# An attention and expert network in one kernel: the rare overflow path moved to the program's end, the row selections of the first expert in another order

## The chip, the cores and the metric

The kernel runs on one core of a Trainium2 chip. The measure is the device time of one execution in microseconds (us). The core has five engines that run their own instruction queues in order and meet at semaphores: TensorE (PE in the profile; PEld is its weight load), VectorE (DVE), ScalarE (ACT), GpSimd (POOL) and SyncE (SP), which here only issues transfers.

## The reference

Three steps follow each other on 1152 tokens of width 512 (2 sequences of 576, 8 heads of 64).

```python
x = attention(q, k, v)          # 4 heads look 32 keys back, 4 at every 32nd key
logits = x @ w_gate             # 8 experts, the best one for each token
gate = softmax(logits)[best]
for token in order:             # an expert takes capacity = 1152 // 8 * 2 = 288 tokens
    keep it if counts[best] < capacity
out1 = gate * (relu(x @ w1[best]) @ w2[best])     # 0 for tokens not kept
out = (sigmoid(out1 @ w_gate2) * (out1 @ w_val)) @ w_out    # 512 -> 1536 -> 512
```

## The kernel before, in words

**Attention and routing.** Twenty units of attention (`attend(i)`) pass through the engines in four stages, their inputs loaded five units ahead. Each finished group of token tiles (128 tokens) is routed (`route_group`, groups of 4, 2, 1, 2 tiles): the best expert, the token's place within that expert's list (a matmul with a triangle of ones and the running counts `accb`), and a write of the token's number into the list `slist` by GpSimd. `route_consts` copies small tables from the second load of constants; it runs after the fourth unit.

**The rows of the first expert** are not gathered from memory but selected on TensorE: `pick_first(t)` multiplies a tile's rows with a 0/1 mask `first` that VectorE makes, and adds into four PSUM tiles `hot`. The rows of the first four tiles are gathered by GpSimd into `xs0` and added by a multiplication with the unit matrix (`pick_first(0)`). The sums are copied to `xd`, split into a rounded high part and a remainder. All matmuls of the expert network work on such pairs: high times high and remainder in one pass of 384 columns, low weight times high in one of 192.

**The expert network** works on `W0` = 192 rows per expert. Its order is written out by hand in `slots`: 64 blocks, four of the first layer ("a", two PSUM halves each) and four of the second ("b") for each expert; the first expert's four "a", then its four "b", from the second expert on an "a" of the next expert between two "b". A block is 16 matmuls. Behind each block the loop emits the evacuation of the block before (`evac`: ScalarE copies one half, VectorE adds the other, ScalarE writes the high part, VectorE the remainder), and the split of a weight chunk four blocks ahead (`split_hi`). "b" blocks are evacuated in pairs of two quarters of the model width. PSUM has four pairs of banks in turn. In the last four blocks the loop also runs steps of `ahead`, which brings the first two pieces of the second network's weights from 64 bits to pairs.

**The overflow path.** An expert with more than 192 tokens has its further rows (up to 96) computed in `overflow`. `values_load` reads the largest count into a register of every engine, and `tc.If(most > W0)` skips the body with a jump. For this input the body is skipped. It stands ahead of the first expert's blocks; it adds its rows into `x2h` and `x2l`, the input of the second network, which the experts then write at offsets `offs` taken from `off_i`. The counts and offsets (`count_offsets`) are made at the seam between routing and experts.

**The second network** makes gate and value for twelve pieces of 128 columns and three token groups of 384 (lines 993 to 995), then multiplies with the output weights tile by tile (nine tiles, lines 1008 to 1010); ScalarE copies a tile out and GpSimd scatters its rows (line 105) by the token list `list_sb`.

Of the kernel before, what the change touches and what calls it, by code (L numbers as in the profile page):

```python
# [20 lines left out]
P = 128  # L21
# [9 lines left out]
WARM = (6, 1)  # L31
AHEAD = 5
# [8 lines left out]
def moe_net_kernel(ctx, tc, cap, S, cst, un, wgate, w1, w2, wgv, wo, out):  # L41
# [51 lines left out]
    tails = list(range(W0, cap, W0))  # L93
    off_i = const.tile([1, E * (1 + len(tails)) + 1], I32, name="off_i")
# [130 lines left out]
    def busy(n):  # L225
        for _ in range(n):
            nc.tensor.matmul(out=warm, lhsT=idle[:, 0:P], rhs=idle, start=True, stop=True)
# [226 lines left out]
    soff = const.tile([P, E], F32, name="soff")  # L454
    mxc = const.tile([P, 1], F32, name="mxc")
    cnt = const.tile([P, E], F32, name="cnt")
    t64 = const.tile([P, E, E], F32, name="t64")
    tne = const.tile([P, NT, E], F32, name="tne")
    cpf = const.tile([P, NT], F32, name="cpf")
    cpi = const.tile([P, NT], I32, name="cpi")  # L460

    def count_offsets():
        cp = ps_tile("ps_o")
        nc.tensor.matmul(out=cp[:, 0:E], lhsT=ones_bf, rhs=accb, start=True, stop=True)
        yield
        nc.vector.tensor_copy(out=cnt, in_=cp[:, 0:E])
        nc.vector.tensor_reduce(out=mxc, in_=cnt, axis=AX.X, op=ALU.max)
        nc.vector.tensor_copy(out=off_i[0:1, E:E + 1], in_=mxc[0:1, :])
        yield
        nc.vector.tensor_tensor(out=t64, in0=below,  # L470
                                in1=cnt.unsqueeze(1).to_broadcast([P, E, E]), op=ALU.mult)
        nc.vector.tensor_reduce(out=soff, in_=t64, axis=AX.X, op=ALU.add)
        nc.vector.tensor_copy(out=off_i[0:1, 0:E], in_=soff[0:1, :])
        for i, c0 in enumerate(tails):
            nc.vector.tensor_scalar(out=off_i[0:1, E + 1 + i * E:E + 1 + (i + 1) * E], in0=soff[0:1, :], scalar1=float(c0),
                                    scalar2=float(N), op0=ALU.add, op1=ALU.min)

    def list_places():
        nc.vector.tensor_tensor(out=tne, in0=oh_all, in1=soff.unsqueeze(1).to_broadcast([P, NT, E]), op=ALU.mult)
        nc.vector.tensor_reduce(out=cpf, in_=tne, axis=AX.X, op=ALU.add)  # L480
        nc.vector.tensor_tensor(out=cpi, in0=cpf, in1=rank_all, op=ALU.add)
# [659 lines left out]
```

## Time and profile before

| | |
|---|---|
| median of three runs | 480.5 us (479.15 to 482.31) |
| profiled execution | 480.65 us, its span 478.9 us |
| TensorE busy | 452.0 us, 94% of the span |
| VectorE, ScalarE, GpSimd busy | 321.6, 241.0, 103.6 us |
| mean granted TensorE clock | 0.972 of full |

The profile is of one execution. Its view of stretches gives, for a piece of the span, how long each engine was busy and which clock TensorE was granted; the timeline gives instructions in order of time, and behind an instruction how long its engine stood idle before it and who released it ("issue" where no releaser shows). A busy TensorE need not run at its full clock.

### The profile page before, as it was taken

Reading aid. Unit: us, or ns where it says so; the run is one execution under the profiler, and the core shown is the slowest. Engines: PE = TensorE matmul, PEld = TensorE weight load, DVE = VectorE, ACT = ScalarE, POOL = GpSimd, SP = SyncE. Lnnn points to the kernel's source line nnn. Section 1 sums busy time; section 2 is a strip of 40 time slices with the busy share of each in tenths; the row PEclk is TensorE's granted clock in tenths of the full one; section 3 lists DMA queues with packets and bytes.
Section 4 is the critical chain, followed back from the end, with each engine's and each line's share of the span. In section 5 each row is a group of like instructions: output and inputs, shape, how many; then the busy total and the mean of one; then the engine's idle time right before and its main releaser. Section 6 shows DMA issues by size and latency. Waiting matters only on the chain.

```text
span 478.9 us, 7652 instructions
## 1 busy us (share of the span) xinstructions
PE 452.0 (94%) x2777; PEld 427.6 (89%) x2777; DVE 321.6 (67%) x625; ACT 241.0 (50%) x513; POOL 103.6 (22%) x97
## 2 busy tenths in 40 slices
PE   7899968699999999999979999999999999999994
PEld 3698867699999999999979999999999998888883
DVE  5489772267787877878778888888888872312110
ACT  4688742256787677767535433434444431313120
POOL 3433613334453844420300000000000000101010
PEclk9899997699999999999989999999999999999998
DMA  8988070497859978768434333334443100101001
GB/s 213 356 241 323 3 275 24 89 325 246 224 202 237 289 227 251 239 201 263 150 115 133 130 125 113 121 127 133 133 131 130 46 1 0 45 22 43 24 27 39
DMA packets 25360, 72.03 MB, mean 150 GB/s; under 512 B 6629, under 2 KB 7013, under 8 KB 25314
## 3 DMA queue, kind: packets, MB, share of 16 engines
q1 hardware_dynamic: 22946, 66.21, 43.6%
q0 software_dynamic: 2368, 5.24, 3.5%
q8 instruction: 24, 0.39, 0.4%
q14 instruction: 22, 0.18, 0.1%
HBM read 65.94 MB, written 5.79 MB: 150 GB/s over the span
## 4 chain that ended last, share of the span: by engine, by line
issue 49%; PE 29%; POOL 2%; DMA 1%; ACT 1%; POOLq 0%; DVE 0%; ACTq 0%
PE ps_p L770 28%; POOL out_dram L105 2%; PE ps_t L752 1%; DMA list_sb<-tlist 1%; POOL wlo L180 0%; POOLq L1137 0%; ACT bs L788 0%; ACT whi L176 0%; DVE ps_p L789 0%; DVE hd L799 0%; ACT hd L793 0%; POOLq L105 0%; POOLq L945 0%; ACTq L788 0%; POOLq L180 0%
## 5 line engine op out<-in xcount | busy, mean ns | idle before, releaser
L993 PE MATMUL ps_q<-x2h,whi 128*128 128x384 f32 x264 | 88.2, 334 | 0.0
L994 PE MATMUL ps_q<-x2l,whi 128*128 128x384 f32 x264 | 88.2, 334 | 0.0
L995 PE MATMUL ps_q<-x2h,wlo 128*128 128x384 f32 x264 | 88.2, 334 | 0.0
L770 PE MATMUL ps_p<-hd,whi 128*128 128x384 f32 x256 | 76.6, 359 | 0.7 <-DVE hd L799 0.7
L176 ACT ACTIVATE whi<-raw 128x1024 fp32r<-128x1024 f32 x60 | 63.5, 1059 | 4.8 <-PE ps_p L770 4.4
L182 DVE TENSOR_TENSOR wlo<-raw,whi 128x1024 fp32r<-128x1024 f32 x52 | 65.5, 1259 | 0.3 <-ACT whi L176 0.3
L770 PE MATMUL ps_p<-hd,wlo 128*128 128x192 f32 x256 | 59.6, 253 | 0.0
L105 POOL DMA_INDIRECT out_dram<-ob,list_sb x9 | 8.8, 980 | 231.4 <-ACT ob L1012 231.4
L993 PEld LDWEIGHTS ps_q<-x2h,whi 128*128 128x128 f32 x264 | 49.6, 188 | 0.0
L994 PEld LDWEIGHTS ps_q<-x2l,whi 128*128 128x128 f32 x264 | 49.6, 188 | 0.0
L995 PEld LDWEIGHTS ps_q<-x2h,wlo 128*128 128x128 f32 x264 | 49.6, 188 | 0.0
L770 PEld LDWEIGHTS ps_p<-hd,whi 128*128 128x128 f32 x256 | 47.8, 189 | 0.9 <-DVE hd L799 0.9
L770 PEld LDWEIGHTS ps_p<-hd,wlo 128*128 128x128 f32 x256 | 48.2, 190 | 0.0
L770 PE MATMUL ps_p<-xd,whi 128*128 128x384 f32 x128 | 41.4, 383 | 5.7 <-issue 5.7
L971 DVE TENSOR_TENSOR wlo<-gv,whi 128x768 fp32r<-128x768 f32 x18 | 16.4, 955 | 44.8 <-ACT whi L970 44.8
L1010 PE MATMUL ps_q<-woh,wlo 128*128 128x512 f32 x108 | 42.0, 389 | 0.0
L1009 PE MATMUL ps_q<-wol,whi 128*128 128x512 f32 x108 | 42.0, 389 | 0.0
L1008 PE MATMUL ps_q<-woh,whi 128*128 128x512 f32 x108 | 42.0, 389 | 0.0
L180 POOL TENSOR_TENSOR wlo<-raw,whi 128x512 fp32r<-128x512 f32 x16 | 26.6, 1685 | 63.3 <-ACT whi L176 63.2
L789 DVE TENSOR_TENSOR ps_p<-ps_p,bs 128x384 f32<-128x384 f32 x48 | 27.0, 562 | 17.8 <-ACT bs L788 16.3
L770 PE MATMUL ps_p<-wol,whi 128*128 128x384 f32 x128 | 37.7, 354 | 0.0
L671 ACT ACTIVATE whi<-mag 128x512 fp32r<-128x512 f32 x22 | 14.0, 635 | 46.0 <-DVE mag L669 46.0
(147 smaller groups left out, 917.3 us busy)
## 6 DMA issues: line engine op xcount, KB each, us to landing
raw<-in_w_dram SPq DMA_DIRECT2D x64, 512.0 KB, 5.2
raw<-in_wgv_dram SPq DMA_DIRECT2D x24, 512.0 KB, 3.5
raw<-in_wo_dram SPq DMA_DIRECT2D x12, 512.0 KB, 3.5
un<-in_un_dram SPq DMA_DIRECT2D x8, 672.0 KB, 7.9
xrows<-xra SPq DMA_DIRECT2D x13, 256.0 KB, 6.1
un<-in_un_dram SPq DMA_DIRECT2D x12, 172.0 KB, 4.9
un<-in_un_dram SPq DMA_DIRECT2D x8, 190.0 KB, 4.1
un<-in_un_dram SPq DMA_DIRECT2D x2, 352.0 KB, 9.0
```

What stands on the lines that cost most here:

```text
L105: ins = nc.gpsimd.indirect_dma_start(in_offset=None, oob_is_err=False, **kw)
L176: nc.scalar.activation(out=hi, in_=raws[j], func=AF.Copy)
L180: nc.gpsimd.tensor_tensor(out=lo[:, sl], in0=raws[j][:, sl], in1=hi[:, sl].bitcast(F32), op=ALU.subtract)
L182: lo_next.append(lambda: nc.vector.tensor_tensor(out=lo, in0=raws[j], in1=hi.bitcast(F32), op=ALU.subtract))
L770: nc.tensor.matmul(start=i == 0 and j == 0, stop=i == n - 1 and j == 1, skip_group_check=True, **kw)
L789: nc.vector.tensor_tensor(out=top, in0=top, in1=bs, op=ALU.add)
L993: nc.tensor.matmul(out=pq[:, 0:TG], lhsT=whv[:, k, fs], rhs=x2h[:, k, gs_], start=k == 0, stop=False)
L994: nc.tensor.matmul(out=pq[:, 0:TG], lhsT=whv[:, k, fs], rhs=x2l[:, k, gs_], start=False, stop=False)
L995: nc.tensor.matmul(out=pq[:, 0:TG], lhsT=wlv[:, k, fs], rhs=x2h[:, k, gs_], start=False, stop=k == ND - 1)
L1008: nc.tensor.matmul(out=pq, lhsT=hv[:, k, :], rhs=woh[:, f, :], start=f == 0, stop=False)
L1009: nc.tensor.matmul(out=pq, lhsT=hv[:, k, :], rhs=wol[:, f, :], start=False, stop=False)
L1010: nc.tensor.matmul(out=pq, lhsT=lv[:, k, :], rhs=woh[:, f, :], start=False, stop=f == NF2 - 1)
```

## The change

The overflow path becomes independent of the main path and moves behind the last tile's matmuls, ahead of the last two output copies: it computes its rows through both networks and scatters them itself. So that nothing of it is needed earlier, `x2h` and `x2l` are filled with zeros in the first four blocks (ScalarE and VectorE), the token numbers in the list are pushed out of range for tokens beyond place 192 (`tok2`), and counts and offsets are made behind the first block. The selection from `xs0` is put last; eight matmuls of zeros are put ahead of the last group's ranks and four behind the last selection. `route_consts` runs after the eighth unit. The first two pieces of the second network are loaded and split earlier, and the last two quarters of the last expert are evacuated one by one.

```diff
+SEAM = (8, 4)
...
-    extras = {3: route_consts, 5: fills}
+    extras = {5: fills, 7: route_consts}
...
     until(g3, "pe")
+    spin = ps_tile("ps_t")
+    busy(SEAM[0], spin)
     until(g3, "acc")
     until(g2)
-    pick_first(0)
     pick_first(N0 + 2)
-    counts = count_offsets()
-    next(counts)
     until(g3)
     pick_first(N0 + 3, N0 + 4)
-    next(counts)
+    pick_first(0)
+    busy(SEAM[1], spin)
...
-    if cap > W0:
-        most = nc.values_load(off_i[0:1, E:E + 1], min_val=0, max_val=N, skip_runtime_bounds_check_because=why)
-        overflow(ps_pair("ps_l"), most)
...
-            out_pp = (kind, e, c, y_pp) if c % 2 else None
+            if e == E - 1 and c >= ND - 2:
+                out_pp = (kind, e, [c], y_pp)
+            else:
+                out_pp = (kind, e, [c - 1, c], y_pp) if c % 2 else None
+        if i == 0:
+            count_offsets()
+        if i < ND and cap > W0:
+            nc.scalar.activation(out=x2h[:, i, 0:N], in_=ones_bf[:, 0:1].to_broadcast([P, N]), func=AF.Copy, scale=0.0)
+            nc.vector.memset(x2l[:, i, 0:N].bitcast(F32), 0.0)
         ev = evac(*done, wmain) if done else iter(())
...
-        if i == 4:
+        if i == 2:
             list_places()
...
-        if kind == "b" and e == E - 1:
-            for _ in range((6, 6, 2, 0)[c]):
-                next(ahead, None)
+        left = len(slots) - i
+        if left in (13, 12):
+            wide_loads(14 - left)
+        for _ in range((0, 2, 2, 2, 2, 2, 1, 1)[left - 1] if left <= 8 else 0):
+            next(ahead, None)
...
+        obs.append((t, pq))
+        if t == NT - 1 and cap > W0:
+            most = nc.values_load(off_i[0:1, E:E + 1], min_val=0, max_val=N, skip_runtime_bounds_check_because=why)
+            overflow()
+        if t != NT - 2:
+            while obs:
+                store_out()
```

How the instructions stand: TensorE at the seam, from the end of the last group's ranks, first before (`xs_93` is the gathered `xs0`, `first` the masks).

```order
L411 LDWEIGHTS ones_bf
L411 MATMUL ps_o<-ohb,ones_bf 128x8
L500 MATMUL ps_s<-front,xs_93 128x96 x6
L500 MATMUL ps_t<-front,xs_93 128x96 x2
L500 MATMUL ps_s<-first,xra 128x192 x3
L500 MATMUL ps_t<-first,xra 128x192
L464 LDWEIGHTS ones_bf
L464 MATMUL ps_o<-accb,ones_bf 128x8
L500 MATMUL ps_s<-first,xra 128x192 x6
L500 MATMUL ps_t<-first,xra 128x192 x2
L883 TENSOR_LOAD off_i
L838 COMPARE_AND_BRANCH
```

And with the change.

```order
L413 LDWEIGHTS ones_bf
L413 MATMUL ps_o<-ohb,ones_bf 128x8
L473 MATMUL ps_s<-first,xra 128x192 x3
L473 MATMUL ps_t<-first,xra 128x192
L473 MATMUL ps_s<-first,xra 128x192 x6
L473 MATMUL ps_t<-first,xra 128x192 x2
L473 MATMUL ps_s<-front,xs_93 128x96 x6
L473 MATMUL ps_t<-front,xs_93 128x96 x2
L229 LDWEIGHTS idle
L229 MATMUL ps_t<-idle 128x512
```

The rows from `xs0` stand behind the three tiles, the count matmul is gone, and matmuls of zeros stand where the register load and the jump were.

VectorE from the start of the first expert's blocks, before: weight splits (`wlo`), the sums (`ps_p`) and remainders (`hd`) of the first evacuations.

```order
L168 TENSOR_TENSOR wlo<-raw,whi 128x512 x2
L789 TENSOR_TENSOR ps_p<-ps_p,bs 128x2x192
L182 TENSOR_TENSOR wlo<-raw,whi 128x1024
L799 SCALAR_TENSOR_TENSOR hd<-ps_p,hd 128x2x192
L789 TENSOR_TENSOR ps_p<-ps_p,bs 128x2x192
L799 SCALAR_TENSOR_TENSOR hd<-ps_p,hd 128x2x192
L789 TENSOR_TENSOR ps_p<-ps_p,bs 128x2x192
L182 TENSOR_TENSOR wlo<-raw,whi 128x1024
L799 SCALAR_TENSOR_TENSOR hd<-ps_p,hd 128x2x192
```

And with the change, from the count's copy on, up to the remainder of the first block (lines 793, 184 and 803 are those of 789, 182 and 799 before).

```order
L622 COPY cnt<-ps_c 128x8
L623 TENSOR_TENSOR t_1191<-below,cnt 128x64
L625 TENSOR_REDUCE soff<-t_1191 128x8
L626 CAST off_i<-soff 1x8
L627 TENSOR_REDUCE mxc<-cnt 128x1
L628 CAST off_i<-mxc 1x1
L869 MEMSET x2l 128x1152
L170 TENSOR_TENSOR wlo<-raw,whi 128x512
L869 MEMSET x2l 128x1152
L793 TENSOR_TENSOR ps_p<-ps_p,bs 128x2x192
L184 TENSOR_TENSOR wlo<-raw,whi 128x1024
L803 SCALAR_TENSOR_TENSOR hd<-ps_p,hd 128x2x192
```

Six small operations for the offsets and two fills stand ahead of the first block's evacuation.

ScalarE at the end of the expert network, before, from the first piece of the second network (`mag`, `woh`) on; `bs` and `x2h` belong to evacuations.

```order
L652 ACTIVATE mag<-raw 128x512
L671 ACTIVATE woh<-mag 128x512
L652 ACTIVATE mag<-raw 128x512
L671 ACTIVATE woh<-mag 128x512
L788 ACTIVATE bs<-ps_p 128x384
L796 ISA
L796 ACTIVATE x2h<-ps_p 128x2x192
L788 ACTIVATE bs<-ps_p 128x384
L796 ISA
L796 ACTIVATE x2h<-ps_p 128x2x192
```

And with the change.

```order
L653 ACTIVATE mag<-raw 128x512
L792 ACTIVATE bs<-ps_p 128x384
L800 ISA
L800 ACTIVATE x2h<-ps_p 128x2x192
L673 ACTIVATE woh<-mag 128x512
L792 ACTIVATE bs<-ps_p 128x192
L800 ISA
L800 ACTIVATE x2h<-ps_p 128x192
L792 ACTIVATE bs<-ps_p 128x192
L800 ISA
L800 ACTIVATE x2h<-ps_p 128x192
```

The two pieces no longer stand together ahead of an evacuation, and the last two quarters are copied with 192 columns each.

## Rows read from the trace of the kernel before

**Rows 1.** The chain of waits, one of four alike (start us, us, what).
```profile
148.78 18.26 PE ps_p L770 x128
```
**Rows 2.** The waits between 15 and 45 us (us in total, times, longest).
```profile
DVE below L251 <- DMA cs<-in_cst_dram: 2.9, 1, 2.9
...
PE ps_t L319 <- POOL pt L310: 1.9, 1, 1.9
```
**Rows 3.** Stretches: length, busy us of PE, PEld, DVE, ACT, POOL; PEclk; DMA share; GB/s.
```profile
20.00:24.00 4.00, 4.00 (x31) 3.46 (x32) 1.56 (x6) 2.58 (x12) 2.61 (x6) 0.73 1.03 318
...
74.00:76.00 2.00, 2.00 (x11) 2.00 (x11) 0.00 (x0) 0.00 (x0) 1.59 (x2) 0.50 0.02 1
...
88.00:90.00 2.00, 2.00 (x8) 1.68 (x7) 0.60 (x1) 0.21 (x1) 0.00 (x0) 0.50 0.25 14
...
96.00:98.00 2.00, 2.00 (x11) 2.00 (x11) 0.35 (x1) 0.88 (x2) 1.77 (x2) 0.68 1.01 367
...
249.00:250.00 1.00, 1.00 (x5) 1.00 (x5) 0.97 (x3) 0.67 (x2) 0.00 (x0) 0.50 0.00 0
...
380.00:440.00 60.00, 60.00 (x292) 52.90 (x291) 21.93 (x30) 16.29 (x26) 3.97 (x4) 1.00 0.05 18
```
**Rows 4.** The timeline at the seam: start us, us, engine, line, operation [idle before <-releaser].
```profile
71.63 0.67 DVE L435 TENSOR_SCALAR first<-cs,sl,gs 128x192 f32<-128x192 f32 x2
...
72.53 2.70 PE L500 MATMUL ps_s<-front,xs 96*128 96x96 f32 x12 [3.43 <-DMA xs<-xrows,idx]
...
81.40 0.81 PE L500 MATMUL ps_t<-first,xra 128*128 128x192 f32 x4
...
83.47 0.15 DVE L475 TENSOR_SCALAR off_i<-soff 1x8 int32<-1x8 f32 x1
...
86.63 0.63 ACT L166 ACTIVATE whi<-raw 128x512 fp32r<-128x512 f32 x1 [2.83 <-issue]
...
87.05 0.69 PE L770 MATMUL ps_p<-xd,whi 128*128 128x384 f32 x1 [4.83 <-issue]
...
90.85 0.69 PE L770 MATMUL ps_p<-xd,whi 128*128 128x384 f32 x1 [0.82 <-issue]
```
**Rows 5.** Prices: timeline at the start, groups of VectorE, the page's groups.
```profile
1.20 2.74 PE L227 MATMUL ps_t<-idle 128*128 128x512 bf16 x6 [1.20 <-DVE zt L221]
...
L198 DVE MEMSET un<- 64x216 f32 x4 | 1.0, 238 | 0.3
...
L220 DVE MEMSET idle<- 128x256 uint32 x1 | 0.3, 272 | 0.9 <-PEq L1130 0.9
...
L176 ACT ACTIVATE whi<-raw 128x1024 fp32r<-128x1024 f32 x60 | 63.5, 1059 | 4.8 <-PE ps_p L770 4.4
L182 DVE TENSOR_TENSOR wlo<-raw,whi 128x1024 fp32r<-128x1024 f32 x52 | 65.5, 1259 | 0.3 <-ACT whi L176 0.3
```
**Rows 6.** The timeline where the first expert's first layer ends.
```profile
101.89 0.49 ACT L788 ACTIVATE bs<-ps_p 128x384 f32<-128x384 f32 x1 [0.52 <-PE ps_p L770]
...
104.15 0.44 PE L770 MATMUL ps_p<-hd,whi 128*128 128x384 f32 x1 [0.68 <-DVE hd L799]
```
**Rows 7.** The timeline between the two networks.
```profile
243.97 0.36 PE L770 MATMUL ps_p<-hd,whi 128*128 128x384 f32 x1
246.99 0.44 PE L993 MATMUL ps_q<-x2h,woh 128*128 128x384 f32 x1 [2.65 <-ACT x2h L796]
...
250.92 0.34 PE L995 MATMUL ps_q<-x2h,wol 128*128 128x384 f32 x1
...
244.58 0.63 ACT L671 ACTIVATE woh<-mag 128x512 fp32r<-128x512 f32 x1 [2.79 <-DVE mag L669]
245.12 0.47 ACT L788 ACTIVATE bs<-ps_p 128x384 f32<-128x384 f32 x1
```
**Rows 8.** The timeline's last instruction, and the drains of the program's last line.
```profile
473.38 0.97 POOL L105 DMA_INDIRECT out_dram<-ob,list_sb  x1 [7.19 <-ACT ob L1012]
...
L1137 POOLq DRAIN  x3: 46/113/4875, 473.1 to 478.6; - x3
```
**Rows 9.** DMA issues between 50 and 110 us, the last number median us to landing.
```profile
slist<-tok_i,si POOLq DMA_INDIRECT x8, 4.3
...
slot_sb<-slist SPq DMA_DIRECT2D x1, 9.0 KB, 4.4
```

More of the change, by code (lines that the diff above doesn't have):

```diff
@@ L92, in moe_net_kernel @@
     xd = wp.tile([P, ND, 2, W0], F32R, tag="xd", name="xd", bufs=1)
-    tails = list(range(W0, cap, W0))
-    off_i = const.tile([1, E * (1 + len(tails)) + 1], I32, name="off_i")
+    CT = cap - W0
+    assert CT <= 96
+    off_i = const.tile([1, E + 1], I32, name="off_i")
     ZR = -(-(E * cap) // P)
@@ L223, in moe_net_kernel, with busy @@
     warm = ps_tile("ps_t")
-    def busy(n):
+    def busy(n, at=None):
         for _ in range(n):
-            nc.tensor.matmul(out=warm, lhsT=idle[:, 0:P], rhs=idle, start=True, stop=True)
+            nc.tensor.matmul(out=warm if at is None else at, lhsT=idle[:, 0:P], rhs=idle, start=True, stop=True)
     busy(WARM[0])
@@ L452, in route_group @@
                 yield
[L454 to L481, printed above, removed]
     picked = []
@@ L626, in moe_net_kernel @@
     after(ins, slots_puts)
-    for _ in counts:
-        pass
     attn.close()
@@ L658, in narrow_steps @@
         lw, hw = rv[:, :, 0], rv[:, :, 1]
[L659 removed]
+        if wd is None:
+            wd = m2a.tile([P, 512], U32, tag="wd", name="wd", bufs=1)
         nc.vector.tensor_scalar(out=wd, in0=hw, scalar1=5, scalar2=2,
@@ L783, in moe_net_kernel, with evac @@
     where = {s: i for i, s in enumerate(slots)}
-    def evac(kind, e, c, pp, w):
-        top = pp[:, :, 0:w]
-        bs = mk.tile([P, 2, W0], F32, tag="bs", name="bs", bufs=3)[:, :, 0:w]
-        nc.scalar.activation(out=bs, in_=pp[:, :, w:2 * w], func=AF.Copy)
+    def evac(kind, e, cs_, pp, w):
+        n = len(cs_)
+        s0 = cs_[0] % 2
+        top = pp[:, s0:s0 + n, 0:w]
+        bs = mk.tile([P, 2, W0], F32, tag="bs", name="bs", bufs=3)[:, 0:n, 0:w]
+        nc.scalar.activation(out=bs, in_=pp[:, s0:s0 + n, w:2 * w], func=AF.Copy)
         nc.vector.tensor_tensor(out=top, in0=top, in1=bs, op=ALU.add)
@@ L912, in moe_net_kernel @@
                 mm_pair(wmain, [(whv[:, k, fs], wlv[:, k, fs], xds[e][:, k]) for k in range(ND)], last_pp[:, q])
-            out_pp = (kind, e, c, last_pp)
+            out_pp = (kind, e, [c * NQ1 + q for q in range(NQ1)], last_pp)
         else:
@@ L999, in moe_net_kernel, with store_out, out_mms @@
     gv_pend.pop()()
-    for t in range(NT):
-        if t + 1 < NT:
-            gsp[t + 1] = gv_split(t + 1)
-        parts = gsp.pop(t)
-        pq = ps_tile("ps_q")
+    obs = []
+    def store_out():
+        t, pq = obs.pop(0)
+        ob = m2a.tile([P, D], F32, tag="mag", name="ob")
+        nc.scalar.activation(out=ob, in_=pq, func=AF.Copy)
+        put(out_puts, "out", out=out, out_offset=bass.IndirectOffsetOnAxis(ap=list_sb[:, t:t + 1], axis=0), in_=ob,
+            bounds_check=N - 1)
+    def out_mms(pq, parts):
         for f in range(NF2):
@@ L1017, in _units @@
+    for t in range(NT):
+        if t + 1 < NT:
+            gsp[t + 1] = gv_split(t + 1)
+        pq = ps_tile("ps_q")
+        out_mms(pq, gsp.pop(t))
+        obs.append((t, pq))
[5 more added lines that the diff above has]
+                store_out()
 def _units(B, S):
```

182 lines of the change are left out of this document (113 added, 69 removed).

## The prediction

> **What bounds the kernel now.** I read the view of stretches first. From 104 us to 244 us and from 251 us to 472 us TensorE is never idle: in the first, eight blocks of weights take 18.26 us, 2.28 us each, and the chain of waits shows only such rows [rows 1]; in the second it is busy in 60.00 of 60 us [rows 3]. Work taken off another engine in these stretches is worth nothing. What can be won lies where TensorE waits, or runs at its lower clock: three places, which I then read in the timeline. In the first, at 12 to 22 us, VectorE stands 2.9 us for the second load of constants, TensorE then 1.9 us for GpSimd's product, which hangs on VectorE [rows 2]; behind it the granted clock falls: 0.73 of full over 20 to 24 us, so at half (1.2 GHz of 2.4) for some 2.2 us of it [rows 3]. The second is the seam between the routing and the first expert. TensorE waits 3.43 us for the gathered rows `xs0`, runs the row selections at half clock, ends them at 82.2 us, and begins the first expert only at 87.05 us; a second hole of 0.82 us follows before 90.85 us [rows 4]. Half clock stands at 74 to 76 us, at 88 to 90 us, and until about 97 us [rows 3]. The third is the seam between the two networks: the last weight matmul of the experts ends at 244.33 us, the next one begins at 246.99 us, and eleven matmuls from there take 3.93 us [rows 7] at half clock [rows 3].
>
> **The change, part by part.** The profiled execution took 480.65 us (span 478.9 us), 0.15 us from the median of the three times, so the sum is made against 480.65 us.
>
> *Constants later (first place).* The five copies and memsets of `route_consts` move from the fourth to the eighth unit, when their load has long landed. VectorE no longer stands 2.9 us; TensorE's wait of 1.9 us behind it goes [rows 2], and with it, as I take it, the half clock behind that wait, worth up to 1.1 us. What is late next is the units' own loads: the DMA share is full there [rows 3], so part is given back. I take **-2.5 us**; the ends are 0 (the loads bind) and -3.5 us. The five operations cost nothing at their new place, where VectorE waits for scores between units.
>
> *The seam up to the first expert.* Two things leave it. The register load, compare and jump over the overflow body: ScalarE shows 2.83 us for them, TensorE 4.83 us, which includes 1.4 us until VectorE's last write of the offsets at 83.62 us [rows 4]. And the wait for `xs0`: the selection from `xs0` now stands last, behind those of the last three tiles. I follow TensorE. Six fillers took 2.74 us at the program's start, as long as 512 columns take at half clock, so 0.45 us each [rows 5]; I take 0.21 us at full clock. Eight of them, 1.7 us, now stand ahead of the rank matmuls of the last group, which ended at 69.1 us (72.53 less 3.43 us, [rows 4]); less the short wait that stood there, these come 1.5 us later. VectorE's count update waits for them and comes 0.9 us later, and so do the masks behind it: the first of the last three at about 71.9 us, the last two, which were done at 72.3 us, at 73.2 us [rows 4]. Three tiles follow, eight passes and about 1.3 us each (four passes take 0.81 us with the tail of the last, [rows 4]): one from 71.9 us, two from 73.2 us, to 75.9 us. Of the sixteen passes from `xs0` twelve took 2.70 us at half clock [rows 4], so all take some 1.8 us at full clock, to 77.6 us, then four fillers to 78.5 us. The first two quarters of the rows are copied out behind the eighth pass, before 78 us. So the first expert begins at 78.5 us and not 87.05 us: 8.5 us.
>
> *The first expert.* What is not needed at the seam now stands here, in front of evacuations. VectorE gets four memsets of 1152 columns, the six offset operations, and five list operations after block 2 in place of three after block 4; ScalarE gets four fills. Two memsets of [rows 5] give 0.85 ns for each further column, so 1.03 us each; ScalarE's 1024 columns take 1.06 us [rows 5], so about 1.17 us each. The Trainium skill (VectorE: DVE Perf Modes, Zero memsets can be issued as uint32 (trn2), and Specifications) gives a memset one cycle per element at 0.96 GHz: by that 1.20 us each and an end 0.7 us later; the rows say 1.03 us, and the sum goes by them. Each of these operations stands ahead of the evacuation of the block before on its queue. VectorE: the count matmul is out at 80.9 us; then offsets 1.3 us (six of some 0.2 us), memset 1.0, half a split 0.6, memset 1.0, sum 0.5, split 1.15 [rows 5], remainder 0.5 and handovers: block 0 is evacuated at 87.1 us. In the same way block 1 at 89.6, block 2 (behind lists, memset, split) at 93.9, block 3 at 95.4 us. TensorE ends blocks 0 to 2 at 85.4 us. Block 3 needs the PSUM pair of block 0 (the count tile takes one of four) and runs 87.1 to 89.4 us. The next block, the first of the second layer, needs the evacuations one by one: half of it to 90.5 us, its third quarter at 93.9 us, its end at 96.0 us. Before, its last quarter began at 104.15 us behind the same chain from ScalarE's copy to VectorE's remainder, 2.3 us long [rows 6], so it ended at 104.7 us. So of the seam **-8.7 us** is left here. The ends: -13.7 us if the added operations hid entirely (78.5 plus five blocks plus the 1.1 us of the last chain), and -5 us if the clock is at half through the selections (3.7 us of them come back). The chain is nearest to the first value, since it is made of rows.
>
> *The clock behind it.* TensorE now waits 1.7 us before block 3 and 3.4 us inside the next. After 1.9 us, 2.66 us and 3.43 us of waiting this trace fell to half [rows 2, 3, 4, 7]; at 103.5 us after 0.7 us it didn't. So part of the following blocks runs at half: 3 us of it costs 1.5 us. I take **+1.5 us**; the ends are 0 and +4.5 us, the latter from the 9 us of half clock behind 87 us.
>
> What follows is covered: the last list write, at about 77.5 us, lands 4.3 us later, the slot table 4.4 us after that [rows 9], the gathers for the second expert at about 94 us; they are wanted at 102 us.
>
> *The seam between the networks.* The two early gate pieces are split at the last eight blocks, not in the last four, and each of the last two quarters is evacuated alone. Now, ScalarE's copy at 245.12 us stood behind a split that waited for VectorE [rows 7]. Then, three quarters are ready when the blocks end, and the first 18 matmuls of the second network need no more; the last quarter's four operations of 192 columns (some 1.6 us with handovers) lie under them. Gone are 2.66 us of waiting and half of 3.93 us. I take 0.2 us off: **-4.4 us**; the ends are -2.5 us (if the splits, of which two steps now stand ahead of a hidden-layer evacuation, hold TensorE for a block) and -4.7 us. The two early loads take two of the four load buffers; the weights behind them come about a block later, and their splits have four blocks to spare.
>
> *The end.* The jump stands before the last two output copies. ScalarE, VectorE, SyncE and GpSimd reach it with 8 us of TensorE's last tile to go, so their jumps are hidden. TensorE's comes after its last matmul, some 4.8 us, beside GpSimd's last scatter and the drain of 4.88 us that the end waits for [rows 8]: **0 us**, with +3 us as the far end.
>
> Sum: -2.5 - 8.7 + 1.5 - 4.4 = -14.1 us, **466.5 us**.
>
> **The rivals.**
> *The clock is lost at the seam.* The fillers don't hold it, the selections run at half and the first expert's stalls draw another 9 us of it: the seam brings 5 us and the clock takes 3 us: 480.65 - 2.5 - 5 + 3 - 4.4 = 471.7 us. For it: the masks still leave TensorE 1.2 us without work at 70.7 us. Against: 0.7 us did no harm.
> *The price of the jump moves to the end.* If TensorE's jump, or GpSimd's wait for all its scatters before it, is on the path, 2.8 to 4.8 us come back: 470.3 us. For it: every engine paid it at the seam. Against: the hiding worked out above. The Trainium skill (Runtime: NRT & Kernel Launch, Instruction fetch mechanics) says that a jump beyond what is prefetched stalls the engine for a fetch, wherever it stands; the 2.83 us of ScalarE agree, and what counts is who waits.
> *It doesn't do all it says.* The unit loads bind at the start (0) and the splits hold the last blocks (-2.5): 480.65 - 7.2 - 2.5 = 470.9 us.
> *Slower.* VectorE stays behind after the first expert, TensorE is interrupted in block after block and stays at 1.2 GHz, where each block costs 2.28 us more. Without the 1.5 us above the sum stands at 465 us; from the seventh such block on the kernel is slower, with ten it takes 487.8 us. For it: VectorE arrives some 5 us late and is busy most of the time. Against: a block at half clock takes 4.6 us, twice VectorE's work, so it would catch up in two or three.
>
> **How the numbers follow.** The forecast has 0.55 (463.5 to 469.5 us by itself), the lost clock 0.20, the jump 0.08, the partial effect 0.13, slower 0.04. The range reaches from 462 us (all ends good but the hidden fills) to 473 us, over the three milder rivals. About 1% (4.8 us) is what a measurement of this kernel tells from no change: faster than 475.8 us has 0.89, with 0.07 for a sum of several bad ends within 1%, and 0.04 slower.
>
> **What would show it.** Right: no wait of VectorE for constants and a clock of 1.00 at 20 to 24 us; the first weight matmul of the experts some 10 us earlier; clock 1.00 in the selections; TensorE waits before block 3 and in the first second-layer block, released by VectorE; no hole between the networks; the drain at the end as long as before. Wrong: half clock at the selections, an end that waits for TensorE's jump, or memsets far from 1.03 us, of which each 0.5 us on all four moves the sum by 1.5 to 2 us.

## The result, and the profile after

The changed kernel took 469.6 us (median of four runs, 469.32 to 469.81), the kernel before beside it 481.36 us (479.15 to 482.31): a ratio of 0.9762, with a 95% interval of 0.9724 to 0.98. The profiled execution took 469.32 us, its span is 467.5 us against 478.9 us. The same kernel was measured twice more, in later groups of runs, each group on a chip of its own beside the kernel before: 476.16 us (472.18 to 477.46, ratio 0.9881, 0.9809 to 0.9954) and 475.5 us (471.6 to 476.75, ratio 0.9913, 0.9885 to 0.9941). So the change is faster in all three, as each interval lies below 1: by 2.4% in the first and by about 1% in the others. Most of the experiments ask what makes this difference between the first measurement and the later two.

Two views of the profile after answer to rows of before. The first is the view of stretches: from:to, length, busy time (and instructions) of TensorE, its weight loads, VectorE, ScalarE and GpSimd, granted clock, DMA share, GB/s.

```profile
16.00:20.00 4.00, 3.86 (x38) 3.52 (x40) 2.42 (x10) 3.91 (x22) 2.11 (x4) 1.00 1.03 400
20.00:24.00 4.00, 3.83 (x40) 3.35 (x38) 3.57 (x11) 2.96 (x16) 2.83 (x7) 1.00 1.04 312
74.00:76.00 2.00, 2.00 (x19) 1.89 (x18) 0.38 (x1) 0.79 (x3) 1.70 (x2) 1.00 0.02 1
90.00:92.00 2.00, 0.00 (x0) 0.00 (x0) 2.00 (x3) 1.70 (x3) 1.58 (x2) 0.92 0.70 203
92.00:94.00 2.00, 1.17 (x4) 1.03 (x4) 1.44 (x4) 0.82 (x2) 1.80 (x2) 0.50 0.55 145
94.00:96.00 2.00, 1.80 (x8) 1.58 (x7) 2.00 (x2) 0.10 (x1) 1.69 (x2) 0.50 0.23 82
96.00:98.00 2.00, 2.00 (x9) 2.00 (x8) 1.79 (x2) 0.95 (x1) 0.00 (x0) 0.50 0.65 156
98.00:100.00 2.00, 2.00 (x13) 2.00 (x13) 0.21 (x1) 0.54 (x1) 0.00 (x0) 0.88 0.95 377
```

The clock of 0.73 at 20 to 24 us [rows 3] is 1.00, and so is the one in the selections (74 to 76 us, 0.50 before). What is left of half clock (1.2 GHz) stands at 92 to 98 us, behind a stretch in which TensorE does nothing and VectorE is busy all the time.

The second view is the timeline of the changed kernel at four places: start, duration, engine and line, output and input, count, and in brackets the idle time before and what ended it.

```profile
68.86 0.17 DVE L420 TENSOR_TENSOR accb<-accb,cn 128x8 bf16<-128x8 bf16 x1 [0.47 <-PE ps_o L413]
...
74.03 1.48 PE L473 MATMUL ps_s<-front,xs 96*128 96x96 f32 x12
75.09 0.78 ACT L593 ACTIVATE xd<-ps_s 128x384 fp32r<-128x384 f32 x2 [2.68 <-PE ps_s L473]
...
76.88 0.44 PE L772 MATMUL ps_p<-xd,whi 128*128 128x384 f32 x1
...
81.01 1.02 DVE L869 MEMSET x2l<- 128x1152 f32 x1 [0.40 <-issue]
...
85.28 0.55 DVE L803 SCALAR_TENSOR_TENSOR hd<-ps_p,hd 128x384 fp32r<-128x384 f32 x1
...
88.66 0.44 PE L772 MATMUL ps_p<-hd,whi 128*128 128x384 f32 x1 [1.72 <-DVE hd L803]
...
89.36 0.17 DVE L638 TENSOR_TENSOR tok<-far,tok_i 128x9 int32<-128x9 f32 x1
...
92.23 0.55 DVE L803 SCALAR_TENSOR_TENSOR hd<-ps_p,hd 128x384 fp32r<-128x384 f32 x1
...
92.83 0.69 PE L772 MATMUL ps_p<-hd,whi 128*128 128x384 f32 x1 [3.36 <-DVE hd L803]
...
93.16 2.53 POOL L182 TENSOR_TENSOR wlo<-raw,whi 128x512 fp32r<-128x512 f32 x2
...
94.29 2.49 DVE L184 TENSOR_TENSOR wlo<-raw,whi 128x1024 fp32r<-128x1024 f32 x1
...
236.54 0.36 PE L772 MATMUL ps_p<-hd,whi 128*128 128x384 f32 x1
236.74 0.34 PE L945 MATMUL ps_q<-x2h,woh 128*128 128x384 f32 x1
...
238.15 0.44 PE L945 MATMUL ps_q<-x2h,woh 128*128 128x384 f32 x1 [0.20 <-ACT x2h L800]
...
460.47 0.39 PE L967 MATMUL ps_q<-woh,wlo 128*128 128x512 f32 x1
460.94 0.60 ACT L957 ACTIVATE ob<-ps_q 128x512 f32<-128x512 f32 x1 [7.56 <-PEq L991]
461.81 0.97 POOL L107 DMA_INDIRECT out_dram<-ob,list_sb  x1 [7.19 <-ACT ob L957]
```

At the first seam TensorE goes from the selections to the first expert at 76.88 us (87.05 us before [rows 4]). In the first expert it waits 1.72 and 3.36 us for VectorE's remainders `hd` (0.68 us once before [rows 6]). Between the networks the hole of 2.65 us [rows 7] is gone: 0.20 us. The last scatter goes out 5.7 us ahead of the end; it was 5.5 us in the kernel before [rows 8].

To compare kernels whose first 60 us differ from run to run, I cut each trace at six events: VectorE's last count update (`accb`, 68.86 us above), the first weight matmul of the experts (76.88), the transposes of the second expert (101.57), the last weight matmul of the experts (236.54), the last matmul (460.47) and the end of the span (467.47). A is from the first to the second, B, C, D and E the next ones, in us, all of the one execution whose trace is kept; "time" is the median of the runs. That execution was the slowest of its kernel in e4, e5 and e6 (477.84, 477.46 and 475.13 us) and the fastest in e3 and e9 (474.79 and 471.6 us), so a trace and a median need not agree.

| kernel | count update | A | B | C | D | E | time |
|---|---|---|---|---|---|---|---|
| before | 69.88 | 17.17 | 22.35 | 134.58 | 228.06 | 6.83 | 481.36 |
| changed | 68.86 | 8.01 | 24.70 | 134.97 | 223.92 | 7.00 | 469.6 |
| e1, no fills | 68.59 | 10.50 | 20.32 | 135.07 | 223.91 | 6.83 | 466.97 |
| e2, fills on GpSimd | 71.23 | 10.31 | 19.78 | 134.99 | 223.91 | 6.83 | 469.46 |
| e3, no filler | 67.01 | 10.61 | 29.48 | 135.04 | 223.93 | 6.83 | 476.17 |
| e4, constants early | 70.00 | 10.59 | 29.62 | 135.04 | 223.91 | 6.83 | 473.78 |
| e5, changed again | 69.19 | 10.49 | 29.91 | 134.94 | 223.91 | 7.23 | 476.16 |
| e6, before without jump | 71.26 | 14.12 | 17.42 | 134.58 | 229.10 | 6.81 | 472.94 |
| e7, xs0 early | 69.00 | 12.49 | 27.25 | 134.99 | 223.93 | 7.22 | 475.62 |
| e8, old second seam | 68.52 | 10.28 | 29.88 | 134.56 | 227.88 | 7.14 | 479.59 |
| e9, changed, third time | 67.38 | 10.45 | 26.15 | 135.09 | 223.91 | 6.83 | 475.5 |
| e10, relieved | 69.05 | 10.31 | 20.70 | 135.04 | 223.91 | 6.83 | 467.75 |
| e11, relieved, xs0 in the middle | 69.85 | 10.20 | 21.47 | 135.09 | 223.91 | 6.83 | 469.28 |
| e12, relieved, no filler | 68.43 | 11.03 | 20.23 | 135.08 | 223.93 | 6.82 | 466.82 |

The groups are e1 to e4 (the kernel before beside them 479.2 us), e5 to e8 (480.27 us) and e9 to e12 (480.0 us). From before to after the span lost 11.4 us: 1.0 before the count update, 9.2 in A, 4.1 in D; B gave back 2.4, C 0.4, E 0.2. Among the others only A and B differ much, but for D in e8, which undoes the second seam, and in e6, where it is 1.0 us longer than before.

### The profile page after: what moved, and what is told of

Its sections match the earlier page's. It is cut to its first block, busy times and chain, and to the rows that moved or that the text cites. A ratio compares the mean times of both kernels' runs of the same rounds, so it can differ in the third digit from the quotient of the medians.

```text
span 467.5 us, 7692 instructions
## 1 busy us (share of the span) xinstructions
PE 448.8 (96%) x2789; PEld 423.6 (91%) x2789; DVE 328.1 (70%) x632; ACT 244.8 (52%) x519; POOL 103.2 (22%) x97
## 4 chain that ended last, share of the span: by engine, by line
issue 47%; PE 37%; DVE 5%; DMA 5%; POOL 3%; ACT 2%; POOLq 0%; SPq 0%; DVEq 0%; ACTq 0%
PE ps_p L772 26%; DMA out_dram<-ob,list_sb 3%; PE ps_s L288 3%; PE ps_t L321 1%; PE ps_s L473 1%; POOL out_dram L107 1%; PE ps_x L368 1%; PE ps_o L335 1%; PE ps_t L754 1%; DMA list_sb<-tlist 1%; DVE x2l L869 1%; DMA un<-in_un_dram 1%; PE ps_o L348 1%; POOL pt L312 1%; ACT pt L299 1%
## 5 line engine op out<-in xcount | busy, mean ns | idle before, releaser
L772 PE MATMUL ps_p<-hd,whi 128*128 128x384 f32 x256 | 79.3, 368 | 5.4 <-DVE hd L803 5.3
L184 DVE TENSOR_TENSOR wlo<-raw,whi 128x1024 fp32r<-128x1024 f32 x52 | 66.7, 1283 | 0.2 <-ACT whi L178 0.2
L772 PE MATMUL ps_p<-hd,wlo 128*128 128x192 f32 x256 | 60.6, 257 | 0.0
L772 PEld LDWEIGHTS ps_p<-hd,whi 128*128 128x128 f32 x256 | 49.1, 194 | 6.5 <-DVE hd L803 6.5
L772 PEld LDWEIGHTS ps_p<-hd,wlo 128*128 128x128 f32 x256 | 49.6, 196 | 0.0
L772 PE MATMUL ps_p<-xd,whi 128*128 128x384 f32 x128 | 37.6, 355 | 0.1
L957 ACT ACTIVATE ob<-ps_q 128x512 f32<-128x512 f32 x9 | 5.4, 598 | 56.5 <-issue 30.5
```

What stands on the lines that cost most here:

```text
L184: lo_next.append(lambda: nc.vector.tensor_tensor(out=lo, in0=raws[j], in1=hi.bitcast(F32), op=ALU.subtract))
L772: nc.tensor.matmul(start=i == 0 and j == 0, stop=i == n - 1 and j == 1, skip_group_check=True, **kw)
```

## The experiments

**e1, the fills left out.** The rows that they zero are all written by an expert with these inputs.

```diff
-        if i < ND and cap > W0:
-            nc.scalar.activation(out=x2h[:, i, 0:N], in_=ones_bf[:, 0:1].to_broadcast([P, N]), func=AF.Copy, scale=0.0)
-            nc.vector.memset(x2l[:, i, 0:N].bitcast(F32), 0.0)
```

> The changed kernel without the eight zero fills of x2h and x2l (left out: the zeroing of rows that no expert writes; with these inputs no such row exists). Theory A, the fills queued ahead of the first expert's evacuations are what the seam gives back: four memsets of 1.02 us on VectorE and the handovers behind ScalarE's fills go, the waits of 1.72 and 3.36 us in the first second-layer block shrink to under 2 us in all, the clock behind it stays up or falls for a shorter time, and the time is 4 to 6 us less, 463.5 to 465.5 us. Rival B, VectorE is late through its weight splits and evacuations anyway (about 2.3 us of them for each block of 2.28 us) and the offset and list operations: the waits stay at 4 us or more and the time is 468 to 469.5 us.

466.97 us (466.54 to 467.07), ratio 0.9742 (0.9714 to 0.977). B is 20.32 us, 4.4 us less than in the changed kernel's own trace and 9.6 us less than in e5's. The waits for `hd` come to 2.1 us for 5.3 us, just over theory A's 2 us. Theory A holds in the stretch that it speaks of; the time came out 1.5 us above its range, and A (the table's) was 2.5 us longer, for a reason that e5 looks into.

**e2, the fills on GpSimd.**

```diff
+    if cap > W0:
+        for i in range(ND):
+            for x in (x2h, x2l):
+                nc.gpsimd.memset(x[:, i, 0:N].bitcast(F32), 0.0)
     fetch(1)
     fetch(2)
```

> The changed kernel with the eight fills as eight memsets on GpSimd, which stands idle from 76.1 to 88.4 us, instead of four on VectorE and four on ScalarE. From the 0.96 us that GpSimd's memset of 96x1024 took, 1.08 us each, 8.6 us in all, out by about 85 to 88 us. Theory A: as without the fills, 463.5 to 466 us. Rival C, GpSimd's memsets slow VectorE's operations beside them or run past 88.4 us and hold the row gathers behind them: VectorE's splits take over 1.3 us for 1.21 us or the second expert's transposes wait, and 467 us or more is left.

469.46 us (467.59 to 470.51), ratio 0.9795 (0.9754 to 0.9835). B is 19.78 us, as without the fills, and eight memsets of 1.06 to 1.09 us on GpSimd leave VectorE's split beside them at 1.20 us. So moving them is as good as leaving them out where they stood. The time is 2.5 us above e1's; in the two traces (1.8 us apart) the count update comes 2.64 us later, and A and B are 0.7 us shorter. The code ahead of it is the same, but for the fillers, in eleven of these traces, and there it comes at 67.0 to 71.2 us. So C falls for the stretch, and the time alone decides neither.

**e3, no filler matmuls.**

```diff
-SEAM = (8, 4)
+SEAM = (0, 0)
```

> The changed kernel without the twelve filler matmuls (8 ahead of the last ranks, 4 behind the last selection). Theory A, the fillers hold TensorE's clock through the wait for VectorE's masks: without them the granted clock falls to half between 68 and 78 us, the selections take up to twice their 0.10 us a pass, and the time is 2 to 4 us more, 471.5 to 473.5 us. Rival D, the order of the selections alone keeps the pauses short and the fillers are only work on the path: the time is 0.5 to 2 us less, 467.5 to 469 us.

476.17 us (474.79 to 476.62), ratio 0.993 (0.9904 to 0.9956). The clock is 1.00 until 76 us and then 0.62 and 0.53, so it did not fall in the selections. A plus B is 40.1 us, in e5, with the fillers and with the same long A, 40.4 us. The time is that of e5. That speaks for D, though not for its 0.5 to 2 us less; e12 asks again. In this timeline one list operation of VectorE took 2.83 us (0.22 us in the changed kernel), and it ended with GpSimd's split:

```profile
91.37 2.83 DVE L634 TENSOR_TENSOR tne<-oh_all,soff 128x72 f32<-128x72 f32 x1
...
91.57 2.52 POOL L182 TENSOR_TENSOR wlo<-raw,whi 128x512 fp32r<-128x512 f32 x2
```

**e4, the constants early again.**

```diff
-    extras = {5: fills, 7: route_consts}
+    extras = {3: route_consts, 5: fills}
```

> The changed kernel with the five constant operations back behind the fourth unit. Theory A, that move brought 1.57 us (the product of the first group's last rows 66.11 to 64.54 us): VectorE stands some 2.9 us for the constants at 15 to 18 us, the clock falls to 0.7 over 20 to 24 us, and the time is 471.0 to 471.5 us. Rival E, the 1.57 us came from other moves ahead of 64 us or are absorbed later: 469.3 to 470 us.

473.78 us (472.25 to 477.84), ratio 0.9876 (0.9833 to 0.9919). VectorE stands 2.5 us for the constants, and the stretches show the clock of before:

```profile
16.00:20.00 4.00, 2.22 (x18) 2.01 (x15) 2.66 (x10) 3.37 (x18) 2.31 (x3) 0.84 1.04 393
20.00:24.00 4.00, 4.00 (x33) 3.26 (x33) 1.95 (x6) 2.19 (x10) 2.17 (x5) 0.73 1.04 295
```

So the mechanism is the one expected. Its size can't be had from this time: A and B are as in e5, and the runs are 5.6 us apart. The count update comes at 69.88, 70.00 and 71.26 us in the three traces with the constants early, at 67.01 to 71.23 us, on average 68.83 us, in the eleven with them late: 1.5 us, within a spread of 4 us. The fillers stand ahead of this event and take part of the gain back: from the count update before it to this one it is 2.77 us in the changed kernel and 2.2 us in the four traces without fillers. At the last matmuls ahead of the fillers (the products with the gate weights, 66.11 us before, 64.54 us in the changed kernel) the gain is 1.57 us, on average over the same traces 1.8 us.

**e5, the changed kernel again.**

> The changed kernel once more, unchanged, beside the others of this group. In the four traces of the first group ScalarE's copy of the first expert's rows began 2.3 to 2.5 us after the selections' passes as the trace has them (in the changed kernel's own trace 0.05 us after). Theory F, that pause belongs to the run or the chip and not to the edits: it shows here too, the first weight matmul stands near 79 us, and the time is 469 to 474 us with a wide spread. Rival G, the edits brought it: no pause, first weight matmul near 76.9 us, 469.3 to 469.9 us.

476.16 us (472.18 to 477.46). The pause shows, and then a second difference that I had not foreseen, both in its timeline:

```profile
74.39 1.48 PE L473 MATMUL ps_s<-front,xs 96*128 96x96 f32 x12
...
75.70 0.61 PE L473 MATMUL ps_t<-front,xs 96*128 96x96 f32 x4
...
77.92 0.71 ACT L593 ACTIVATE xd<-ps_s 128x384 fp32r<-128x384 f32 x2 [5.15 <-PE ps_t L229]
...
79.68 0.42 PE L772 MATMUL ps_p<-xd,whi 128*128 128x384 f32 x1 [2.50 <-DVE xd L594]
...
93.75 3.19 DVE L638 TENSOR_TENSOR tok<-far,tok_i 128x9 int32<-128x9 f32 x1
...
94.41 2.49 POOL L182 TENSOR_TENSOR wlo<-raw,whi 128x512 fp32r<-128x512 f32 x2
...
97.12 1.02 DVE L869 MEMSET x2l<- 128x1152 f32 x1 [0.18 <-issue]
...
100.24 0.69 PE L772 MATMUL ps_p<-hd,whi 128*128 128x384 f32 x1 [6.30 <-DVE hd L803]
```

From the first pass over `xs0` to ScalarE's first copy it is 3.53 us (74.39 to 77.92), in the changed kernel's first trace 1.06 us (74.03 to 75.09): TensorE then waits 2.50 us for the rows. Theory F holds, since the code is the same, though the time lies above its 469 to 474 us. The semaphore events of the trace say on which side the pause lies: ScalarE starts 0.02 us behind the first of four updates by TensorE at 77.90, 77.96, 78.02 and 78.08 us, which in the first trace come at 75.07, 75.52, 75.97 and 76.83 us. So ScalarE isn't slow, the updates are late, and they come closer together than the work that they report (the four fillers alone take 1.03 us). Then VectorE's last list operation, 0.17 us in the first trace, takes 3.19 us: it began 0.66 us ahead of the row of GpSimd's split and ends at 96.94 us, when that split ends (96.90 us). Behind it in the queue stand a memset and the evacuations of blocks 2 and 3, and TensorE waits 6.30 us and not 3.36 us, and runs at half clock until about 107 us (0.50 over 96 to 104 us, 0.59 over 104 to 108). GpSimd's split comes behind its four row gathers, which wait for the slot table, not for TensorE: the first starts 1.03 us behind the table's landing in both traces, 19.5 and 19.6 us behind the count update. The pause moves VectorE 2.5 us later against the split, and that lets the two meet.

**e6, the kernel before without its jump.** Left out is the second pass for tokens beyond 192 of an expert.

```diff
-    if cap > W0:
-        most = nc.values_load(off_i[0:1, E:E + 1], min_val=0, max_val=N, skip_runtime_bounds_check_because=why)
-        overflow(ps_pair("ps_l"), most)
```

> The kernel before without the register load, the compare and the overflow body at the seam (left out: the second pass over tokens beyond 192 of an expert, which these inputs don't have). Theory A, the jump's price at the seam is what ScalarE and TensorE stood there: 2.83 us on ScalarE's path plus part of the half clock behind it, so 3.5 to 5.5 us less than the kernel before, a ratio of 0.989 to 0.993. Rival H, the second wait, for VectorE's evacuations, grows by what the first loses: less than 1.5 us is won, ratio over 0.997.

472.94 us (471.95 to 475.13), ratio 0.9835 (0.9776 to 0.9894): 7.3 us, more than A expected, and H falls. A is 3.05 us shorter, near the 2.83 us that ScalarE stood [rows 4]; B is 4.93 us shorter, because TensorE meets one wait of 0.68 us there instead of the hole and the half clock of before [rows 3, 4]:

```profile
85.38 0.44 PE L770 MATMUL ps_p<-xd,whi 128*128 128x384 f32 x1 [0.81 <-DVE xd L621]
...
97.13 0.44 PE L770 MATMUL ps_p<-hd,whi 128*128 128x384 f32 x1 [0.68 <-issue]
```

The edit takes the register load, the compare, the jump, the body's instructions and the PSUM pair that the body holds away together, so what each of them costs isn't shown. Together they are worth 8.0 us in A and B, and the whole change brings 6.8 us there in its best trace (A 9.16 less, B 2.35 more). In its group the median of this kernel lies 3.2 us below that of the changed one, though their runs overlap.

**e7, the selection from `xs0` early.**

```diff
+    pick_first(0)
     pick_first(N0 + 2)
     until(g3)
     pick_first(N0 + 3, N0 + 4)
-    pick_first(0)
```

> The changed kernel with the selection from the gathered rows xs0 back ahead of the last three tiles. Theory A, TensorE waits for xs0 there as before: xs0 lands some 3 us after GpSimd issued the second gather (69.6 us), so the passes start near 72.7 us and not 70.0 us, the clock falls to half behind a pause of over 3 us, and the time is 4 to 6 us more than the changed kernel of this group. Rival I, the eight fillers cover the wait and only the order differs: 0 to 2 us more.

475.62 us (473.22 to 478.26), within the spread of e5. TensorE waits 2.32 us for `xs0` and the clock falls to half, as A has it:

```profile
71.30 2.66 PE L473 MATMUL ps_s<-front,xs 96*128 96x96 f32 x12 [2.32 <-DMA xs<-xrows,idx]
```

A is 2.0 us longer than in e5 (12.49 against 10.49), not 4 to 6: the pause before ScalarE's copies is missing here. And B is 2.7 us shorter, so that A and B together are 39.74 us here and 40.40 us in e5. The new order of the selections is worth 4.5 us in A where the pause stays away (12.49 less 8.01); where it comes, the 2.0 us of A are gone again in B, and the medians (475.62 and 476.16 us) show no gain either.

**e8, the seam between the networks as before.**

```diff
-        left = len(slots) - i
-        if left in (13, 12):
-            wide_loads(14 - left)
-        for _ in range((0, 2, 2, 2, 2, 2, 1, 1)[left - 1] if left <= 8 else 0):
-            next(ahead, None)
+        if kind == "b" and e == E - 1:
+            for _ in range((6, 6, 2, 0)[c]):
+                next(ahead, None)
...
-            if e == E - 1 and c >= ND - 2:
-                out_pp = (kind, e, [c], y_pp)
```

> The changed kernel with the seam between the networks as before: both early gate pieces split in the last expert's second layer, loaded there, and the last two quarters evacuated together. Theory A, this seam alone brought 4.1 us (11.56 us earlier at the last matmul, 7.43 us at the last weight matmul of the experts): a wait of 2.65 us and half clock behind it come back, and the time is 3.8 to 4.4 us more than the changed kernel of this group. Rival J, part of it was won elsewhere: under 2.5 us more.

479.59 us (477.82 to 480.24), 3.4 us above e5, a little under theory A's range; D is 3.97 us longer, within it. The wait is back, as long as before:

```profile
243.24 0.36 PE L772 MATMUL ps_p<-hd,whi 128*128 128x384 f32 x1
...
246.28 0.69 PE L942 MATMUL ps_q<-x2h,woh 128*128 128x384 f32 x1 [2.68 <-ACT x2h L800]
```

Theory A holds, and J falls. C is 134.56 us here, as in the two kernels with the old schedule, and 134.94 to 135.09 us in the others: the early splits cost 0.4 us in the blocks.

**e9, the changed kernel a third time.**

> The changed kernel unchanged, as the measure for the others of this group. Theory F, the pause of some 2.4 us between the selections and the first weight matmul comes and goes with the run or chip: either 8.0 us from the last count update to the first weight matmul and 24.7 us from there to the second expert's transposes (469 to 470 us), or 10.5 us and 29.5 to 29.9 us (474 to 477 us).

475.5 us (471.6 to 476.75). The pause is there (A 10.45 us), B is a third case, 26.15 us:

```profile
90.27 0.20 DVE L638 TENSOR_TENSOR tok<-far,tok_i 128x9 int32<-128x9 f32 x1
...
91.25 2.49 POOL L182 TENSOR_TENSOR wlo<-raw,whi 128x512 fp32r<-128x512 f32 x2
...
92.05 2.79 DVE L184 TENSOR_TENSOR wlo<-raw,whi 128x1024 fp32r<-128x1024 f32 x1
...
95.36 0.69 PE L772 MATMUL ps_p<-hd,whi 128*128 128x384 f32 x1 [4.94 <-DVE hd L803]
```

The list is through, and a weight split of VectorE meets GpSimd, with block 2's remainder behind it. In the first trace (B 24.70) the split that met GpSimd stood behind all remainders. So F's two cases are at least three, by which of VectorE's operations meets GpSimd's split: a list operation in all five traces with B over 27 us (2.82 to 3.19 us in e3, e4, e5, e7 and e8; e7 has no pause, its selections end late by themselves), a weight split in the others of the changed order, e9 among them. No run moves GpSimd's split itself, so its price is read from these traces.

**e10, VectorE relieved.** The fills as in e2, and:

```diff
+    count_offsets()
     for i, (kind, e, c) in enumerate(slots):
...
-        if i == 0:
-            count_offsets()
...
-        if i == 2:
+        if i == 4:
             list_places()
```

> The changed kernel with the fills on GpSimd, the count matmul ahead of the first expert's first block and the list operations behind block 4. Theory A, VectorE's lateness at the first evacuations sets the stretch from the first weight matmul to the second expert's transposes: with nothing else queued there it takes 17.4 to 18.5 us (17.42 us in the kernel before without its jump; 24.7 us in the changed kernel, 29.9 us with the pause), with or without the pause, and the time is 464 to 467 us. Rival B, the splits and evacuations alone keep VectorE late: 19.5 us or more and 467 to 469 us.

467.75 us (467.31 to 469.2), ratio 0.9759 (0.9728 to 0.979), 7.8 us below e9 beside it. B is 20.70 us: above the 17.4 to 18.5 us of theory A, and no better than e2's 19.78 us, so that moving the count and the lists brought nothing that shows beyond the fills. B and the time lie where rival B has them, but not for its reason, as the timeline shows:

```profile
83.83 1.06 POOL L832 MEMSET x2h<- 128x1152 f32 x1
84.52 1.22 DVE L184 TENSOR_TENSOR wlo<-raw,whi 128x1024 fp32r<-128x1024 f32 x1
...
90.95 1.06 ACT L178 ACTIVATE whi<-raw 128x1024 fp32r<-128x1024 f32 x1 [2.38 <-DMA raw<-in_w_dram]
...
92.42 0.56 DVE L803 SCALAR_TENSOR_TENSOR hd<-ps_p,hd 128x384 fp32r<-128x384 f32 x1 [2.12 <-ACT hd L797]
...
93.04 0.44 PE L772 MATMUL ps_p<-hd,whi 128*128 128x384 f32 x1 [1.59 <-DVE hd L803]
...
93.67 2.52 POOL L182 TENSOR_TENSOR wlo<-raw,whi 128x512 fp32r<-128x512 f32 x2
...
94.68 2.61 DVE L184 TENSOR_TENSOR wlo<-raw,whi 128x1024 fp32r<-128x1024 f32 x1
```

VectorE isn't late here. It stands 2.12 us for ScalarE, and ScalarE 2.38 us for a chunk of weights from memory, which had been asked for only at 84.81 us: it stood in SyncE's queue behind the load of the slot table, which waits 4.1 us for the list writes to land (0.2 us in e6, where the first expert starts later). In e2 and e12 ScalarE stands 2.63 and 0.95 us for the same chunk, in e6 (B 17.42 us) not at all. The rest of B is half clock behind the pause (0.59 at 80 to 84 us). This is read from the traces; no run moves that load. VectorE's split meets GpSimd's here too (94.68 us), but behind the last remainder, where nobody waits for it.

**e11, `xs0` between the third last tile and the last two.** As e10, and:

```diff
     pick_first(N0 + 2)
+    pick_first(0)
     until(g3)
     pick_first(N0 + 3, N0 + 4)
-    pick_first(0)
```

> As the relieved kernel, with the selection from xs0 between the third last tile and the last two. Theory K, the pause before ScalarE's copies hangs on the passes over xs0 standing last (none in the kernel before and in the changed kernel with that selection early): it is gone and 8 to 9 us lie between the last count update and the first weight matmul, plus what TensorE waits for xs0 (landed 2.5 us after the count update, so about 0.5 us). Rival L, the pause hangs on the run: 10 to 10.6 us here as in the others of this group that show it.

469.28 us (468.65 to 469.89), ratio 0.9784 (0.9757 to 0.9812). A is 10.20 us: the pause is there although the passes over `xs0` don't stand last. K falls.

**e12, the relieved kernel without fillers** (the edit of e3 on e10).

> As the relieved kernel, without the twelve filler matmuls. Theory A, without them the clock falls at the wait for the masks or behind the pause and the first expert starts at half clock: 2 to 4 us more than the relieved kernel. Rival D, once VectorE isn't late the fillers are worth nothing, as between the two kernels with the pause (39.4 us from count update to transposes with fillers, 40.1 us without): within 1.5 us of the relieved kernel.

466.82 us (466.31 to 467.32), ratio 0.9728 (0.9703 to 0.9754), the fastest that computes everything: 8.7 us below the changed kernel beside it and 13.2 us below the kernel before. The clock falls earlier (0.76 at 76 to 80 us, 0.50 at 80 to 84), A is 0.7 us longer, B 0.5 us shorter. Theory A falls, D holds: where the pause comes, the fillers bring nothing. (For the 39.4 us that D names with fillers the traces of e4, e5 and e8 have 40.2 to 40.4 us.) Whether they hold the clock where it doesn't, no run shows, since the changed kernel's first trace is the only one of its order without it.

## Why the prediction was right, point by point

The forecast of 466.5 us stood 3 us below the 469.6 us measured first. In spans it had 14.1 us and the trace shows 11.4 us.

*Constants.* The mechanism is right: no wait of VectorE for `cs`, clock 1.00, and both come back in e4. The size is not: 1.57 us ahead of the fillers (1.8 us on average over fourteen traces) for 2.5 us, of which 1.0 us is left at the count update behind them. The low end's reason, that the units' loads bind, may hold in part: the DMA share is still 1.03 at 16 to 20 us.

*The seam up to the first expert.* 8.5 us was forecast with the fillers ahead of the count update in it; A is 9.16 us shorter, 8.6 us less their 0.56 us, and each step shows: last passes over `xs0` at full clock, fillers behind them, the copies under way. In the ten later traces with this order or that of e11 the pause takes 2.2 to 3.0 us of it back.

*The first expert.* The queue of VectorE was worked out well. Counted from the first weight matmul, the blocks were to be evacuated after 8.6, 11.1, 15.4 and 16.9 us; they were after 8.95, 11.73, 15.90 and 17.49 us (remainders' ends 85.83, 88.61, 92.78, 94.37 us, less 76.88). The memsets took 1.02 us, near the 1.03 us that [rows 5] gave; the 1.20 us worked out from the Trainium skill (VectorE: DVE Perf Modes, Zero memsets can be issued as uint32 (trn2), and Specifications) isn't borne out. One step was wrong: block 3 did not wait for the PSUM pair of block 0. The wait came one block later, 1.72 us, before the second quarter that reads block 1's remainder; the sum of the waits is 5.28 us, for 5.1 us.

*The clock behind it.* 1.5 us was forecast for 3 us of work at half. The stretches have 5.4 us of it (1.17, 1.80 and 2.00 us at 92 to 98 us, and 0.48 us of the 0.88 stretch), so 2.7 us. That is 1.2 us more, and covers the 1 us by which B missed: 17.5 us to the end of the next block, 4.7 us more to the transposes (104.7 to 109.40 us before) and 1.5 us make 23.7 us, and it took 24.70 us.

*The seam between the networks.* 4.4 us forecast, 4.14 us in D, 3.97 us back in e8. The first 18 matmuls did not run through, as the prediction has it: 0.20 us of waiting stands ahead of the seventh. The price named beside it, splits that hold a block, is there with 0.4 us in C.

*The end.* 0 us forecast, 0.17 us measured (E; 6.8 to 7.2 us in all traces, so within their spread). The jump beside TensorE's last tile costs nothing that shows.

*The range.* Its lower end, 462 us, doesn't come out of the ends named: without lost clock they sum to -3.5 - 8.7 - 4.7 = -16.9 us, so some 464 us.

*The rivals.* In the first measurement none came true. In the two later ones something like the first did, at another place: the selections keep their clock, the pause comes behind them, VectorE meets GpSimd, and the clock falls in the first expert; 475.5 and 476.16 us lie outside the range. That the first measurement met the forecast is therefore in part luck: the sum has no term for the pause and none for VectorE meeting GpSimd, and in that measurement's trace the one is missing and the other does no harm. The prediction had counted each VectorE operation at the duration that it has alone, and had not asked what GpSimd does then, though its gathers and its split were in the timeline of before. What the change removed was worth more than I took: the jump with its body 8.0 us by itself (e6). What it put in its place, the fills in front of the evacuations, gave back 4.4 to 4.9 us of B in the good case and 9 to 10 us in the bad one (24.70, and 29.5 to 29.9, against 19.78 and 20.32 us). Nor had it asked when the first expert's weights arrive, which go out behind the slot table's load and set part of what is left (e10).

What stays open is the pause: between TensorE's passes and ScalarE's first copy, in all ten traces of the later groups with the changed order or that of e11, not in the changed kernel's first trace, and in none of the three with the selection from `xs0` ahead of the last three tiles. It does not come from the fills, the fillers, the constants, the second seam or the last place of the passes over `xs0`, each of which was taken away or moved. In all ten TensorE's updates that release ScalarE's copies come 0.06 us apart, in the other four traces 0.45 to 0.65 us apart; what holds the updates back nothing here shows.

## What to carry to other kernels

Work taken out of a stall must be put where the engine is idle and nobody waits behind it: the same zero fills cost 4.4 us and more in front of evacuations and nothing that shows on an idle GpSimd. When operations move, lay the queues of VectorE and GpSimd side by side, not each alone: one 0.17 us operation that meets a 2.5 us one can move everything behind it. When a stage starts 10 us earlier, ask when its loads go out and what stands ahead of them in their queue. And cut the traces at common events before comparing: the same code came 4 us apart at the count update, which hides differences of 2 us in the time.

## What the hardware showed that I had not expected

VectorE stands while GpSimd's split runs. Operations with two inputs from SBUF that met it took 3.19 us for 0.17 (e5), 2.83 for 0.22 (e3), and the weight split 2.49 to 2.79 us for 1.21 (the changed kernel, e9, e10), each ending just after the split did or its own duration later (the two small ones had begun 0.66 and 0.20 us ahead of the split's own row). It holds both ways: in the later blocks of the changed kernel's trace a weight split of VectorE that starts 0.04 us behind GpSimd's takes 2.33 us, and one that starts 0.02 us ahead of it takes its usual 1.22 us and GpSimd's 2.34 us for 1.29 us. Evacuations that read PSUM (0.54 to 0.57 us) ran beside it unhindered, and so did the split beside GpSimd's memsets (1.22 us). The Trainium skill (SBUF — State Buffer, SBUF: two separate sides) says that the two engines share a port pair under an exclusive lock, which a VectorE operation with two SBUF inputs needs only against a GpSimd operation that reads SBUF; the traces agree on both halves.

Waits of one length before the first weight matmul did not have one effect on the clock: behind 2.50 us (e5), 2.54 us (e1) and 2.32 us (e10) it was 0.58 to 0.61 over 80 to 84 us, behind 2.49 us (e9) and 2.35 us (e2) it stayed at 1.00.
